# Moving one store to ScalarE's DMA queue, and two new ways to close the output tiles

## The chip, the cores and the metric

The kernel runs on one core of a Trainium2 chip. The metric is device time in microseconds (us). A "span" is the length of the profiled execution from its first to its last record; it is 1.7 to 3.6 us shorter than the device time of the same run in the runs here, mostly about 2. Engines are named as in the profile: PE is TensorE's matmul, PEld its weight load, DVE is VectorE, ACT is ScalarE, POOL is GpSimd, SP is SyncE, and a name with a small q is the engine's own instruction queue.

## The reference, cut to what matters

```python
x = A_x                                                  # 1 x 2048 x 1024, bf16
g = sigmoid((x * gate_w).sum(-1, keepdims=True))
a = irfft2(rfft2(x) * (w_r + 1j * w_i))                  # branch A: a spectral filter
Bu = einsum("bld,pd->blp", x, B_bar)                     # branch B: a diagonal state space
h = scan(h_t = Lam_bar * h_{t-1} + Bu_t)
b = 2.0 * einsum("blp,dp->bld", h, Cmat).real + x * Dskip
return g * a + (1 - g) * b                               # 1 x 2048 x 1024, bf16
```

The output has 16 row tiles of 128 tokens. Branch B's result for the first ten tiles is ready long before branch A's, so it is parked in DRAM (the "early" tiles). The last six are finished in one go (the "own" tiles).

## The kernel before

The **front end** has 16 steps. In each, TensorE turns x (`turn_x`), multiplies it (`fd`), ScalarE evicts it, TensorE multiplies again (`s1`), VectorE (in the last six steps ScalarE) evicts that as A, and A is stored to a DRAM scratch. B and C arrive by DMA transposes of SyncE's queue meanwhile. From step 8 on, products with B come between.

```python
def load_B(jb):
    for ri, src in enumerate((B_B_re, B_B_im)):
        nc.sync.dma_start_transpose(out=BT[jb][:, ri], in_=src[P * jb:P * (jb + 1), :])

def s1(j):
    ...                                                  # four matmuls into psa
    A1 = gta.tile([P, 2, K], BF16, name="A1", bufs=3)
    (nc.vector.tensor_copy if j < 10 else nc.scalar.copy)(out=A1, in_=psa)
    ...
    nc.sync.dma_start(out=turn1_dram[j].rearrange("r m k -> m r k"), in_=A1)
```

The **back end** closes tiles. `spectral` makes branch A's tile in a buffer: eight matmuls, a ScalarE copy and four VectorE steps. Own tiles use the two halves of a buffer called raw in turn; early tiles use the buffers of B, which is no longer needed.

```python
def late_tile(tb, yl):                                   # an early tile; yl was loaded from DRAM
    ga, _ = spectral(tb, gB, flat(BT[4 + tb % 4]))
    nc.vector.tensor_add(out=ga, in0=yl, in1=ga)
    nc.sync.dma_start(out=out2[P * tb:P * (tb + 1), :], in_=ga.rearrange("p h n -> p (h n)"))

def own_tile(tb, ga):
    psy = psA.tile([P, D], FP32, name="ps_y", tag="ps")
    ga, o = ga
    for hf in range(2):
        c_half(psy, tb, hf, ga)                          # product with C; ga joins by an identity matmul
        if hf == 0:
            load_xs(tb + 1)                              # DMA transpose of the next tile's x, on SyncE
            yield "half"
    nc.scalar.activation(out=o..., in_=psy, func=ACT.Copy, scale=omg[:, tb:tb + 1])
    nc.sync.dma_start(out=out2[P * tb:P * (tb + 1), :], in_=o...)
    yield 3.9
```

The order on TensorE, VectorE and ScalarE is as written; that of SyncE and GpSimd is chosen by the scheduler. The scheduler also hands completion semaphores round among the DMAs of SyncE and ScalarE: eight in the traces of the kernel before (100, 102, 103 and 105 to 109).

Of the kernel before, what the change touches and what calls it, by code (L numbers as in the profile page):

```python
# [11 lines left out]
ACT = mybir.ActivationFunctionType  # L12
ALU = mybir.AluOpType
FP32 = mybir.dt.float32
BF16 = mybir.dt.bfloat16
# [5 lines left out]
D = 1024  # L21
K = 512
H = K // 2
P = 128
TC = 256
NCH = S // TC
NEARLY = 10
NHA, NHB = 4, 2

MAGIC = 12582912.0  # L30
# [75 lines left out]
def kernel(  # L106
# [17 lines left out]
    nc = tc.nc  # L124
    x = A_x[0]
    out2 = out[0]
# [12 lines left out]
    turn1_dram = dram.tile([16, 2, P, K], BF16, name="turn1_scratch")  # L139
    turn2_dram = dram.tile([32, P, K], BF16, name="turn2_scratch")  # L140
    col0_dram = dram.tile([P, 16, 2], BF16, name="col0_scratch")
    z_dram = dram.tile([P, 16], FP32, name="z_scratch")
    y_dram = dram.tile([NEARLY, 2, P, K], FP32, name="y_scratch")

# [16 lines left out]
    gta = ictx.enter_context(tc.tile_pool(name="gta", bufs=2, side="right"))  # L161
    psA = ctx.enter_context(tc.tile_pool(name="psA", bufs=2, space=PSUM, reuse_waits="tile"))
# [11 lines left out]
    ident = cpool.tile([P, P], BF16, name="ident")  # L174
# [7 lines left out]
    BT = [btp.tile([P, 2, 8, P], BF16, name=f"BT{jb}") for jb in range(8)]  # L182
# [12 lines left out]
    def load_T3(a, b):  # L195
        nc.sync.dma_start(out=fft["T3"][:, a:b], in_=cT3[:, a:b])

    def load_B(jb):
        for ri, src in enumerate((B_B_re, B_B_im)):
            nc.sync.dma_start_transpose(out=BT[jb][:, ri], in_=src[P * jb:P * (jb + 1), :])  # L200


    def make_tab(jp):
# [32 lines left out]
    hs = {}  # L236
# [85 lines left out]
    def gfnet():  # L322
        T3_sb, G_sb = fft["T3"], fft["G"]
        Acol = fx.tile([P, 16, 2], BF16, name="Acol")
# [11 lines left out]
        def s1(j):  # L336
            X1 = X1s.pop(j)
            psa = psA.tile([P, 2, K], FP32, name="ps_s1", tag="ps")
            nc.tensor.matmul(psa[:, 0, :], lhsT=T3_sb[:, j, 0, :], rhs=X1[:, 0, :], start=True, stop=False)
            nc.tensor.matmul(psa[:, 0, :], lhsT=T3_sb[:, j, 1, :], rhs=X1[:, 1, :], start=False, stop=True)  # L340
            nc.tensor.matmul(psa[:, 1, :], lhsT=T3_sb[:, j, 0, :], rhs=X1[:, 1, :], start=True, stop=False)
            nc.tensor.matmul(psa[:, 1, :], lhsT=T3_sb[:, j, 2, :], rhs=X1[:, 0, :], start=False, stop=True)
            A1 = gta.tile([P, 2, K], BF16, name="A1", bufs=3)
            (nc.vector.tensor_copy if j < 10 else nc.scalar.copy)(out=A1, in_=psa)  # L344
            if j:
                nc.vector.tensor_copy(out=Acol[:, j - 1, :], in_=A1s[j - 1][:, :, 0])
            A1s[j] = A1
            nc.sync.dma_start(out=turn1_dram[j].rearrange("r m k -> m r k"), in_=A1)

        A1s, X1s = {}, {}  # L350
        fft["fd"], fft["s1"] = fd, s1
        yield "front"
        nc.vector.tensor_copy(out=Acol[:, 15, :], in_=A1s[15][:, :, 0])
        nc.gpsimd.dma_start(out=col0_dram, in_=Acol)
        Bcol = fx.tile([P, 16, 2], BF16, name="Bcol")
        with nc.allow_non_contiguous_dma(reason="tiny corner turn"):
# [77 lines left out]
        for h in range(2):  # L434
            for ri in range(2):
                nc.tensor.matmul(qps[:, h, :], lhsT=fft["Sel"][:, 2 * h + ri, :], rhs=Qb[:, :, ri],
                                 start=(ri == 0), stop=(ri == 1))
# [46 lines left out]
        for G in range(8):  # L484
# [3 lines left out]
            for kp in range(2):  # L488
                psz = psA.tile([P, 2, K], FP32, name="ps_is2", tag="ps")
                for kl in range(2):  # L490
                    kc = 2 * kp + kl
                    pv = psz[:, kl, :].rearrange("p (n t) -> p n t", t=8)
                    for g in range(4):
                        nc.tensor.matmul(pv[:, :, g::4], lhsT=Cq[:, g, P * kc:P * (kc + 1)], rhs=KRS_sb[:, 1, :],  # L494
                                         start=True, stop=True)
                nc.scalar.copy(out=ZT[:, 4 * kp:4 * kp + 4, :, 8 * G:8 * G + 8],  # L496
                               in_=psz.rearrange("p kc (r n t) -> p (kc r) n t", r=2, t=8))
# [27 lines left out]

    bctx = ExitStack()
    gen = gfnet()

    def step():
# [10 lines left out]
    xs = {}  # L540

    def load_xs(tb):
        if tb < 16:
            xs[tb] = fft["lp"].tile([P, 8, P], BF16, name="xs", bufs=2)
            nc.sync.dma_start_transpose(out=xs[tb], in_=x[P * tb:P * (tb + 1), :])

    def c_half(psy, tb, dh, ga=None):
        c, tq = tb // 2, tb % 2
        vector_until(c)
        for i in range(16):  # L550
            jb, ri = i // 2, i % 2
            nc.tensor.matmul(psy[:, 512 * dh:512 * (dh + 1)], lhsT=hs[c, jb // 4][:, ri, jb % 4, P * tq:P * (tq + 1)],  # L552
                             rhs=CT[ri][:, jb, 512 * dh:512 * (dh + 1)], start=(i == 0), stop=False)
        for d4 in range(4):
            d8 = 4 * dh + d4
            nc.tensor.matmul(psy[:, P * d8:P * (d8 + 1)], lhsT=xs[tb][:, d8, :],  # L556
                             rhs=fft["dgD"][:, d8, :], start=False, stop=(d4 == 3 and ga is None))
        if ga is not None:
            nc.tensor.matmul(psy[:, 512 * dh:512 * (dh + 1)], lhsT=ident, rhs=ga[:, dh], start=False, stop=True)

    def early(tb):
        psy = pools["u"].tile([P, D], FP32, name="ps_y", tag="psu")
# [11 lines left out]
    own_home = lambda tb: raw[:, 2 * D * (tb % 2):2 * D * (tb % 2 + 1)]  # L574
    flat = lambda t: t.rearrange("p r j m -> p (r j m)")

    def spectral(tb, scale, home):
        ZT_t = fft["ZT"]
        pse = pools["u"].tile([P, 4, H], FP32, name="ps_id", tag="psu")
        for slot, (cls, ri) in enumerate(((0, 0), (1, 1), (0, 1), (1, 0))):  # L580
            for kb in range(2):
                i = 4 * cls + 2 * kb + ri
                nc.tensor.matmul(pse[:, slot, :], lhsT=ZT_t[:, i, tb, :], rhs=fft["Gi"][:, i, :],  # L583
                                 start=(kb == 0), stop=(kb == 1))
        part = home[:, 0:D].rearrange("p (s c n) -> p s c n", s=2, c=2)
        nc.scalar.activation(out=part.rearrange("p s c n -> p (s c) n"), in_=pse, func=ACT.Copy, scale=scale[:, tb:tb + 1])  # L586
        eo = home[:, D:2 * D].rearrange("p (c k) -> p c k", c=2)
        nc.vector.tensor_add(out=eo[:, :, 0:H], in0=part[:, 0], in1=part[:, 1])
        nc.vector.tensor_sub(out=eo[:, :, K - 1:H - 1:-1], in0=part[:, 0], in1=part[:, 1])
        ga = part.rearrange("p s c n -> p s (c n)")  # L590
        nc.vector.tensor_add(out=ga[:, 0], in0=eo[:, 0], in1=eo[:, 1])
        nc.vector.tensor_sub(out=ga[:, 1], in0=eo[:, 0], in1=eo[:, 1])
        return ga, eo

    def late_load(tb):
        yl = flat(BT[tb % 4]).bitcast(FP32).rearrange("p (h n) -> p h n", h=2)
        nc.sync.dma_start(out=yl, in_=y_dram[tb].rearrange("h p n -> p h n"))
        return yl

    def late_tile(tb, yl):  # L600
        ga, _ = spectral(tb, gB, flat(BT[4 + tb % 4]))
        nc.vector.tensor_add(out=ga, in0=yl, in1=ga)
        nc.sync.dma_start(out=out2[P * tb:P * (tb + 1), :], in_=ga.rearrange("p h n -> p (h n)"))

    def own_tile(tb, ga):
        psy = psA.tile([P, D], FP32, name="ps_y", tag="ps")
        ga, o = ga
        for hf in range(2):
            c_half(psy, tb, hf, ga)
            if hf == 0:  # L610
                load_xs(tb + 1)
                yield "half"
        nc.scalar.activation(out=o.rearrange("p h n -> p (h n)"), in_=psy, func=ACT.Copy, scale=omg[:, tb:tb + 1])
        nc.sync.dma_start(out=out2[P * tb:P * (tb + 1), :], in_=o.rearrange("p h n -> p (h n)"))
        yield 3.9


    preTs = {}
# [5 lines left out]
        nc.scalar.copy(out=xQ[:, :, j, :], in_=pt)  # L624

    def fold(j):
        preTs[j] = gta.tile([P, 8, P], BF16, name="preT", bufs=4)
        nc.vector.tensor_add(out=preTs[j][:, 0:4], in0=xQ[:, 0:4, j, :], in1=xQ[:, 4:8, j, :])
        nc.vector.tensor_sub(out=preTs[j][:, 4:8], in0=xQ[:, 0:4, j, :], in1=xQ[:, 4:8, j, :])

    idle = gta.tile([P, K], BF16, name="idle", tag="A1", bufs=3)
    nc.vector.memset(idle, 0.0)

    def keep_warm(n):
# [21 lines left out]
    rows = iter(range(2, 16))  # L656
# [26 lines left out]
    gB = cpool.tile([P, 16], FP32, name="gB")  # L683
    omg = cpool.tile([P, 16], FP32, name="omg")
    grat = cpool.tile([P, 16], FP32, name="grat")
# [34 lines left out]
    def halves(gen, n):  # L720
# [6 lines left out]
                early(8), unit(6, 0), early(9))  # L727

    order = {
        **{j: [(load_B, j - 2)] for j in range(2, 10)},  # L730
        10: [(load_small,)],
        **{j: [(load_C, j - 11)] for j in range(11, 15)},
    }
    at = [0]
# [91 lines left out]
    while at[0] < 16:  # L826
        j = at[0]
# [43 lines left out]
    for _ in ssm:  # L871
        vector(3.5)
    assert step() is None
    yl, ga = {}, {}
    late = list(range(NEARLY))

    def own(tb):
        for v in own_tile(tb, ga.pop(tb)):
            if v == "half" and tb + 1 < 16:
                ga[tb + 1] = spectral(tb + 1, grat, own_home(tb + 1))  # L880
            yield v

    ga[NEARLY] = spectral(NEARLY, grat, own_home(NEARLY))
    for _ in chain(unit(6, 1), unit(7, 0), unit(7, 1)):
        vector(4.0)
    for i in range(4):
        yl[i] = late_load(i)
    for tb, counts in ((10, (0, 0)), (11, (1, 1)), (12, (1, 1)), (13, (1, 1)), (14, (1, 1)), (15, (2, 0))):
        for _, n in zip(own(tb), counts):
            vector(4.0)  # L890
            for _ in range(n):
                i = late.pop(0)
                late_tile(i, yl.pop(i))
                if i + 4 < NEARLY:
                    yl[i + 4] = late_load(i + 4)
    guard.__exit__(None, None, None)


# [28 lines left out]
```

## Time and profile before

| | before |
|---|---|
| device time, median of 3 | 359.76 us (359.44 to 360.09) |
| span | 357.5 us |
| TensorE busy | 342.6 us, 96% |
| VectorE busy | 302.4 us, 85% |
| first product with B starts | 46.94 us |
| second half of it starts | 54.69 us |
| TensorE's last product ends | 352.41 us |

The kernel is close to TensorE's own work. A change can win only what TensorE lacks.

### The profile page before, as it was taken

What the parts mean: (1) busy time and instruction counts of PE and PEld (TensorE: products, weight loads), DVE (VectorE), ACT (ScalarE), POOL (GpSimd) and SP (SyncE); (2) the same over time, 40 slices, a digit from 0 to 9 for tenths busy, and PEclk for the clock granted to TensorE, in tenths of its full rate; (3) what the DMA queues carried; (4) which work ended last, traced back from release to release, by engine and by line L of the source; (5) the groups of instructions that cost most, each with busy time, mean ns of one, the idle gap of its engine ahead of it and who ended that gap; (6) DMA issues with size and microseconds to landing.
All of it is one profiled execution on the core that took longest, in us unless ns stands there. A gap on an engine that the chain in (4) does not pass through costs nothing.

```text
span 357.5 us, 6458 instructions
## 1 busy us (share of the span) xinstructions
PE 342.6 (96%) x2533; PEld 227.8 (64%) x2533; DVE 302.4 (85%) x483; ACT 170.2 (48%) x217; POOL 23.2 (6%) x56
## 2 busy tenths in 40 slices
PE   8989689989999999999999999999999999999994
PEld 4545257757876665665657486597767875665661
DVE  2658385999998999999999999956747998999996
ACT  3698555674432265566646333364423222434432
POOL 1373010120021000000000000000000000000000
PEclk9999989999999999999999999999999999999999
DMA  7999999997592068899999276863203241145673
GB/s 266 415 233 165 239 214 196 225 185 181 185 225 54 38 131 202 213 282 254 253 274 254 82 187 173 200 158 110 88 2 91 64 172 43 33 132 149 206 264 120
DMA packets 83455, 62.18 MB, mean 174 GB/s; under 512 B 54336, under 2 KB 71392, under 8 KB 83296
## 3 DMA queue, kind: packets, MB, share of 16 engines
q1 hardware_dynamic: 82832, 61.70, 67.1%
q0 software_dynamic: 512, 0.05, 0.5%
q8 instruction: 20, 0.33, 0.4%
q14 instruction: 11, 0.09, 0.1%
q10 hardware_dynamic: 80, 0.01, 0.0%
HBM read 31.32 MB, written 17.84 MB: 138 GB/s over the span
## 4 chain that ended last, share of the span: by engine, by line
PE 79%; DVE 7%; ACT 4%; SPq 4%; issue 3%; DMA 3%; ACTq 0%; DVEq 0%
PE ps_y L552 29%; PE psu L295 29%; PE ps_is L494 4%; PE ps_id L583 3%; SPq L200 3%; PE ps_fd L330 3%; PE ps_is L469 2%; PE ps_is L470 2%; PE ps_s L445 2%; PE ps_y L556 2%; DMA G_sb<-c_G 2%; ACT xQ L624 1%; DVE A L344 1%; DMA turn_scratch<-A 1%; ACT h L297 1%
## 5 line engine op out<-in xcount | busy, mean ns | idle before, releaser
L295 PE MATMUL psu<-xQ,BT 128*128 128x256 bf16 x1024 | 117.5, 275 | 1.8 <-ACT zsb L667 1.0
L552 PE MATMUL ps_y<-CT,h 128*128 128x512 bf16 x512 | 115.9, 379 | 0.0
L295 PEld LDWEIGHTS <-BT 128*128 128x128 bf16 x1024 | 101.1, 99 | 18.1 <-issue 2.5
L552 PEld LDWEIGHTS <-h 128*128 128x128 bf16 x512 | 50.2, 99 | 55.2
L269 DVE TENSOR_TENSOR_SCAN h<-rz,h 128x1024 bf16<-128x1024 f32 x32 | 72.3, 2282 | 0.3
L297 ACT CAST h<-psu 128x1024 bf16<-128x1024 f32 x32 | 32.3, 1010 | 60.7 <-PE psu L295 60.7
L256 DVE TENSOR_TENSOR su<-h,tab 128x2048 bf16<-128x2048 bf16 x16 | 19.6, 1223 | 16.4 <-ACT h L297 13.3
L330 PE MATMUL ps_fd<-G_sb,preT 128*128 128x512 bf16 x128 | 30.4, 379 | 0.5 <-ACT X L333 0.3
L570 ACT ACTIVATE ye<-ps_y,omg 128x512 f32<-128x512 f32 x20 | 12.7, 685 | 31.2 <-PE ps_y L556 25.2
L344 DVE CAST A<-ps_s 128x1024 bf16<-128x1024 f32 x10 | 12.2, 1223 | 11.2 <-DMA turn_scratch<-A 6.8
L330 PEld LDWEIGHTS <-preT 128*128 128x128 bf16 x128 | 11.9, 97 | 13.6 <-issue 1.2
L257 DVE TENSOR_TENSOR h<-h,tab 128x2048 bf16<-128x2048 bf16 x16 | 19.6, 1225 | 1.0
L496 ACT CAST ZT<-ps_is 128x1024 bf16<-128x1024 f32 x16 | 15.4, 1020 | 10.3 <-PE ps_is L494 6.7
L333 ACT CAST X<-ps_fd 128x1024 bf16<-128x1024 f32 x16 | 16.2, 1013 | 8.5 <-PE ps_fd L330 8.4
L282 DVE TENSOR_TENSOR h<-h,tab 128x2048 bf16<-128x2048 bf16 x16 | 19.6, 1225 | 0.5
L447 ACT CAST X<-ps_s 128x1024 bf16<-128x1024 f32 x16 | 16.2, 1014 | 7.0 <-PE ps_s L445 7.0
L281 DVE TENSOR_TENSOR sg<-h,tab 128x2048 bf16<-128x2048 bf16 x16 | 19.5, 1219 | 0.1
L472 ACT CAST C<-ps_is 128x1024 bf16<-128x1024 f32 x16 | 16.1, 1007 | 2.8 <-PE ps_is L470 2.8
L624 ACT COPY xQ<-pt 128x1024 bf16<-128x1024 bf16 x16 | 15.9, 1019 | 2.1 <-PE pt L623 2.1
L583 PE MATMUL ps_id<-raw,ZT 128*128 128x256 bf16 x128 | 15.8, 273 | 0.0
L586 ACT ACTIVATE raw<-ps_id,grat 128x1024 bf16<-128x1024 f32 x6 | 6.7, 1114 | 18.1 <-PE ps_id L583 18.1
L494 PE MATMUL ps_is<-KRS_sb,raw 128*128 128x128 bf16 x128 | 15.3, 311 | 0.0
(187 smaller groups left out, 397.4 us busy)
## 6 DMA issues: line engine op xcount, KB each, us to landing
y_scratch<-ye SPq DMA_DIRECT2D x20, 256.0 KB, 2.7
BT<-y_scratch SPq DMA_DIRECT2D x10, 512.0 KB, 4.1
CT<-in_A_x_dram SPq DMA_DIRECT2D x8, 512.0 KB, 6.5
turn_scratch<-A SPq DMA_DIRECT2D x16, 256.0 KB, 2.9
Bb<-turn_scratch SPq DMA_DIRECT2D x16, 256.0 KB, 4.1
turn_scratch<-C SPq DMA_DIRECT2D x16, 256.0 KB, 3.3
raw<-turn_scratch SPq DMA_DIRECT2D x16, 256.0 KB, 4.2
Wb<-in_A_w_r_dram SPq DMA_DIRECT2D x32, 127.8 KB, 4.3
```

Of the source, the lines that this page charges most:

```text
L256: nc.vector.tensor_mul(out=su, in0=u[:, ::-1], in1=bc(1))
L257: nc.vector.tensor_mul(out=u, in0=u, in1=bc(0))
L269: nc.vector.tensor_tensor_scan(out=seg, data0=rz[:, js].rearrange("p j t -> p (j t)"), data1=seg, initial=0.0, op0=ALU.mult, op1=ALU.add)
L281: nc.vector.tensor_mul(out=sg, in0=u[:, ::-1], in1=bc(3))
L282: nc.vector.tensor_mul(out=u, in0=u, in1=bc(2))
L295: nc.tensor.matmul(psu[:, j, :], lhsT=BT[4 * q + j][:, ri, d8, :], rhs=xQ[:, d8, :, 16 * c:16 * (c + 1)], start=(d8 == 0), stop=(d8 == 7))
L297: nc.scalar.copy(out=u[:, ri].rearrange("p b (q j) -> p b q j", j=16), in_=psu.rearrange("p b (j q) -> p b q j", j=16))
L330: nc.tensor.matmul(ps[:, cls, :], lhsT=preTs[j][:, 4 * cls + d4, :], rhs=G_sb[:, cls, d4, :], start=(d4 == 0), stop=(d4 == 3))
L494: nc.tensor.matmul(pv[:, :, g::4], lhsT=Cq[:, g, P * kc:P * (kc + 1)], rhs=KRS_sb[:, 1, :], start=True, stop=True)
L552: nc.tensor.matmul(psy[:, 512 * dh:512 * (dh + 1)], lhsT=hs[c, jb // 4][:, ri, jb % 4, P * tq:P * (tq + 1)], rhs=CT[ri][:, jb, 512 * dh:51 ...
L583: nc.tensor.matmul(pse[:, slot, :], lhsT=ZT_t[:, i, tb, :], rhs=fft["Gi"][:, i, :], start=(kb == 0), stop=(kb == 1))
L624: nc.scalar.copy(out=xQ[:, :, j, :], in_=pt)
```

## The change

Its intent: take the A stores away from SyncE's queue, where they stand between B's transposes; relieve VectorE of the ten late sums; and shorten the end. The diff, cut to its core:

```diff
-    def load_B(jb):
-        for ri, src in enumerate((B_B_re, B_B_im)):
-            nc.sync.dma_start_transpose(out=BT[jb][:, ri], in_=src[...])
+    parts_B = iter([(jb, ri) for q in range(2) for ri in range(2) for jb in range(4 * q, 4 * q + 4)])
+    def load_B(n):
+        for _ in range(n):
+            jb, ri = next(parts_B)
+            nc.sync.dma_start_transpose(out=BT[jb][:, ri], in_=(B_B_re, B_B_im)[ri][...])
...
-            A1 = gta.tile([P, 2, K], BF16, name="A1", bufs=3)
+            A1 = gta.tile([P, 2, K], BF16, name="A1", bufs=4)
...
-            nc.sync.dma_start(out=turn1_dram[j].rearrange("r m k -> m r k"), in_=A1)
+            if j:
+                keep_A1(j - 1)
+        def keep_A1(j):
+            nc.vector.tensor_copy(out=Acol[:, j, :], in_=A1s[j][:, :, 0])
+            nc.scalar.dma_start(out=turn1_dram[j].rearrange("r m k -> m r k"), in_=A1s[j])
...
-    def late_tile(tb, yl):
-        ga, _ = spectral(tb, gB, flat(BT[4 + tb % 4]))
-        nc.vector.tensor_add(out=ga, in0=yl, in1=ga)
-        nc.sync.dma_start(out=out2[...], in_=ga...)
+    def late_tile(tb):
+        ga, _ = spectral(tb, gB, flat(BT[tb % 8]))
+        nc.gpsimd.dma_start(out=ga, in_=y_dram[tb]..., accum_op=ALU.add)
+        closing.append((tb, ga))                         # stored one tile later, from SyncE's queue
...
+        if tb < NSUM:                                    # NSUM = 13: own tiles 10 to 12 as before
...                                                      # own tiles 13 to 15:
         for hf in range(2):
+            psh = psA.tile([P, K], FP32, name="ps_h", tag="ps")
+            c_half(psh, tb, hf)                          # no identity matmul
+            nc.vector.scalar_tensor_tensor(out=o[:, hf], in0=psh, scalar=omg[:, tb:tb + 1], in1=ga[:, hf],
+                                           op0=ALU.mult, op1=ALU.add)
+            nc.sync.dma_start(out=out2[rows, K * hf:K * (hf + 1)], in_=o[:, hf])
...
-        **{j: [(load_B, j - 2)] for j in range(2, 10)},
-        10: [(load_small,)],
+        **{j: [(load_B, n)] for j, n in ((2, 1), (3, 1), (4, 1), (5, 2), (6, 2), (7, 2), (8, 2), (9, 2))},
+        10: [(load_B, 3), (load_small,)],
```

Each A is now stored one step late (`keep_A1(j - 1)`). The cut parts give the turned x one buffer less (preT, 4 to 3) and start the late tiles one own tile earlier.

More of the change, by code (lines that the diff above doesn't have):

```diff
@@ L27 @@
 NEARLY = 10
+NSUM = 13
 NHA, NHB = 4, 2
@@ L196, in load_T3 @@
         nc.sync.dma_start(out=fft["T3"][:, a:b], in_=cT3[:, a:b])
-    def load_B(jb):
-        for ri, src in enumerate((B_B_re, B_B_im)):
-            nc.sync.dma_start_transpose(out=BT[jb][:, ri], in_=src[P * jb:P * (jb + 1), :])
+    parts_B = iter([(jb, ri) for q in range(2) for ri in range(2) for jb in range(4 * q, 4 * q + 4)])
+    def load_B(n):
+        for _ in range(n):
+            jb, ri = next(parts_B)
+            nc.sync.dma_start_transpose(out=BT[jb][:, ri], in_=(B_B_re, B_B_im)[ri][P * jb:P * (jb + 1), :])
     def make_tab(jp):
@@ L342, in s1 @@
             nc.tensor.matmul(psa[:, 1, :], lhsT=T3_sb[:, j, 2, :], rhs=X1[:, 0, :], start=False, stop=True)
-            A1 = gta.tile([P, 2, K], BF16, name="A1", bufs=3)
+            A1 = gta.tile([P, 2, K], BF16, name="A1", bufs=4)
             (nc.vector.tensor_copy if j < 10 else nc.scalar.copy)(out=A1, in_=psa)
+            A1s[j] = A1
             if j:
-                nc.vector.tensor_copy(out=Acol[:, j - 1, :], in_=A1s[j - 1][:, :, 0])
-            A1s[j] = A1
-            nc.sync.dma_start(out=turn1_dram[j].rearrange("r m k -> m r k"), in_=A1)
+                keep_A1(j - 1)
+        def keep_A1(j):
+            nc.vector.tensor_copy(out=Acol[:, j, :], in_=A1s[j][:, :, 0])
+            nc.scalar.dma_start(out=turn1_dram[j].rearrange("r m k -> m r k"), in_=A1s[j])
         A1s, X1s = {}, {}
@@ L352, in gfnet @@
         yield "front"
-        nc.vector.tensor_copy(out=Acol[:, 15, :], in_=A1s[15][:, :, 0])
+        keep_A1(15)
         nc.gpsimd.dma_start(out=col0_dram, in_=Acol)
@@ L547, in c_half @@
     def c_half(psy, tb, dh, ga=None):
+        psy = psy[:, K * dh:K * (dh + 1)] if psy.shape[1] == D else psy
         c, tq = tb // 2, tb % 2
@@ L551, in c_half @@
             jb, ri = i // 2, i % 2
-            nc.tensor.matmul(psy[:, 512 * dh:512 * (dh + 1)], lhsT=hs[c, jb // 4][:, ri, jb % 4, P * tq:P * (tq + 1)],
+            nc.tensor.matmul(psy, lhsT=hs[c, jb // 4][:, ri, jb % 4, P * tq:P * (tq + 1)],
                              rhs=CT[ri][:, jb, 512 * dh:512 * (dh + 1)], start=(i == 0), stop=False)
@@ L555, in c_half @@
             d8 = 4 * dh + d4
-            nc.tensor.matmul(psy[:, P * d8:P * (d8 + 1)], lhsT=xs[tb][:, d8, :],
+            nc.tensor.matmul(psy[:, P * d4:P * (d4 + 1)], lhsT=xs[tb][:, d8, :],
                              rhs=fft["dgD"][:, d8, :], start=False, stop=(d4 == 3 and ga is None))
         if ga is not None:
-            nc.tensor.matmul(psy[:, 512 * dh:512 * (dh + 1)], lhsT=ident, rhs=ga[:, dh], start=False, stop=True)
+            nc.tensor.matmul(psy, lhsT=ident, rhs=ga[:, dh], start=False, stop=True)
     def early(tb):
@@ L593, in spectral, with close @@
         return ga, eo
-    def late_load(tb):
-        yl = flat(BT[tb % 4]).bitcast(FP32).rearrange("p (h n) -> p h n", h=2)
-        nc.sync.dma_start(out=yl, in_=y_dram[tb].rearrange("h p n -> p h n"))
-        return yl
-    def late_tile(tb, yl):
-        ga, _ = spectral(tb, gB, flat(BT[4 + tb % 4]))
-        nc.vector.tensor_add(out=ga, in0=yl, in1=ga)
-        nc.sync.dma_start(out=out2[P * tb:P * (tb + 1), :], in_=ga.rearrange("p h n -> p (h n)"))
+    def late_tile(tb):
+        ga, _ = spectral(tb, gB, flat(BT[tb % 8]))
+        nc.gpsimd.dma_start(out=ga, in_=y_dram[tb].rearrange("h p n -> p h n"), accum_op=ALU.add)
+        closing.append((tb, ga))
+    closing = []
+    def close(keep):
+        while len(closing) > keep:
+            tb, ga = closing.pop(0)
+            nc.sync.dma_start(out=out2[P * tb:P * (tb + 1), :], in_=ga.rearrange("p h n -> p (h n)"))
     def own_tile(tb, ga):
-        psy = psA.tile([P, D], FP32, name="ps_y", tag="ps")
         ga, o = ga
-        for hf in range(2):
-            c_half(psy, tb, hf, ga)
+        rows = slice(P * tb, P * (tb + 1))
+        if tb < NSUM:
+            psy = psA.tile([P, D], FP32, name="ps_y", tag="ps")
+            for hf in range(2):
+                c_half(psy, tb, hf, ga)
+                if hf == 0:
+                    load_xs(tb + 1)
+                    yield "half"
+            nc.scalar.activation(out=o.rearrange("p h n -> p (h n)"), in_=psy, func=ACT.Copy, scale=omg[:, tb:tb + 1])
+            nc.sync.dma_start(out=out2[rows, :], in_=o.rearrange("p h n -> p (h n)"))
+            yield 3.9
+            return
+        for hf in range(2):
+            psh = psA.tile([P, K], FP32, name="ps_h", tag="ps")
[3 more added lines that the diff above has]
+            nc.sync.dma_start(out=out2[rows, K * hf:K * (hf + 1)], in_=o[:, hf])
             if hf == 0:
@@ L612, in own_tile @@
                 yield "half"
-        nc.scalar.activation(out=o.rearrange("p h n -> p (h n)"), in_=psy, func=ACT.Copy, scale=omg[:, tb:tb + 1])
-        nc.sync.dma_start(out=out2[P * tb:P * (tb + 1), :], in_=o.rearrange("p h n -> p (h n)"))
         yield 3.9
@@ L626, in fold @@
     def fold(j):
-        preTs[j] = gta.tile([P, 8, P], BF16, name="preT", bufs=4)
+        preTs[j] = gta.tile([P, 8, P], BF16, name="preT", bufs=3)
         nc.vector.tensor_add(out=preTs[j][:, 0:4], in0=xQ[:, 0:4, j, :], in1=xQ[:, 4:8, j, :])
         nc.vector.tensor_sub(out=preTs[j][:, 4:8], in0=xQ[:, 0:4, j, :], in1=xQ[:, 4:8, j, :])
-    idle = gta.tile([P, K], BF16, name="idle", tag="A1", bufs=3)
+    idle = gta.tile([P, K], BF16, name="idle", tag="A1", bufs=4)
     nc.vector.memset(idle, 0.0)
@@ L873 @@
     assert step() is None
-    yl, ga = {}, {}
+    ga = {}
     late = list(range(NEARLY))
@@ L879, in own @@
             if v == "half" and tb + 1 < 16:
-                ga[tb + 1] = spectral(tb + 1, grat, own_home(tb + 1))
+                ga[tb + 1] = spectral(tb + 1, grat if tb + 1 < NSUM else gB, own_home(tb + 1))
             yield v
@@ L885 @@
         vector(4.0)
-    for i in range(4):
-        yl[i] = late_load(i)
-    for tb, counts in ((10, (0, 0)), (11, (1, 1)), (12, (1, 1)), (13, (1, 1)), (14, (1, 1)), (15, (2, 0))):
+    for tb, counts in ((10, (1, 1)), (11, (1, 1)), (12, (1, 1)), (13, (1, 1)), (14, (1, 1)), (15, (0, 0))):
         for _, n in zip(own(tb), counts):
@@ L891 @@
             for _ in range(n):
-                i = late.pop(0)
-                late_tile(i, yl.pop(i))
-                if i + 4 < NEARLY:
-                    yl[i + 4] = late_load(i + 4)
+                close(1)
+                late_tile(late.pop(0))
+            if tb == 15:
+                close(0)
     guard.__exit__(None, None, None)
```

## The prediction

Two passages with general statements, which no trace of this case shows, are cut from it. No term of its sum stood in them: 359.8 + 8 + 0.7 + 3 - 1.8 = 369.7, and 366.5 after 3.3 is taken back. What it says of semaphores agrees with the trace of the kernel before: of the DMAs of SyncE and ScalarE there, 89 have a predecessor on the same semaphore whose landing the trace tells, and none was issued before that landing. Its 0.22 us for an identity product is the step between 128x512 products in that trace (starts at 41.06, 41.28 and 41.49 us).

> **What bounds the kernel now.** I read the page first: its busy shares, its row for TensorE and its chain of the work that ended last.
>
> ```profile
> span 357.5 us, 6458 instructions
> PE   8989689989999999999999999999999999999994
> PE 79%; DVE 7%; ACT 4%; SPq 4%; issue 3%; DMA 3%; ACTq 0%; DVEq 0%
> ```
>
> TensorE is the chain for 79% of the span and is full from the sixth of the 40 slices (some 9 us each) to the last. Time is to be won only where its row falls short: the first 50 us, the worst being the fifth slice, and the last 5 us. The chain in order of time and TensorE's own timeline tell what it lacks in the fifth slice:
>
> ```profile
> 36.94 0.53 SPq L348
> 37.52 1.28 SPq L200
> 38.84 1.31 SPq L200
> 40.19 1.31 SPq L200
> 41.60 3.09 DMA turn_scratch<-A
> 44.80 1.24 DVE A L344
> 46.08 0.38 PE ps_s L339
> 47.11 5.16 PE psu L295 x32
> ...
> 41.06 0.38 PE L339 MATMUL ps_s<-X,raw 128*128 128x512 bf16 x1 [2.42 <-DVE A L344]
> 46.08 0.38 PE L339 MATMUL ps_s<-X,raw 128*128 128x512 bf16 x1 [2.27 <-DVE A L344]
> ```
>
> The store of the first token result (L348) stands in SyncE's queue behind B's transposes (L200, 1.3 us of issue each). VectorE can't write the next A until an old store has landed, and TensorE waits for VectorE twice. TensorE's real gaps are 38.3 to 41.1 and 43.4 to 46.1, some 5.4 us. The first B product after them took 5.2 us where later ones take 3.5 to 3.7, so about 1.6 us more is a lowered clock (0.85 in that window by the busy time by stage). Together 7 us are at stake here.
>
> At the end the timeline shows the last product stopping at 352.41 us, then eviction, VectorE's sums and stores:
>
> ```profile
> 348.36 3.62 PE L552 MATMUL ps_y<-CT,h 128*128 128x512 bf16 x16
> 352.03 0.38 PE L559 MATMUL ps_y<-raw,ident 128*128 128x512 bf16 x1
> 353.19 1.23 DVE L602 TENSOR_TENSOR BT<-BT,BT 128x1024 bf16<-128x1024 f32 x1
> 354.45 0.33 SPq L603 DMA_DIRECT2D out_dram<-BT x1
> ```
>
> That tail is 357.5 - 352.4 = 5.1 us. The busy time by stage has TensorE at 20.00 of 20 from 280 to 340 us beside VectorE at 18 to 19.5: VectorE is full, but TensorE never waits for it there.
>
> [...] This build has eight hardware-DMA semaphores handed round, and each DMA waits first until the last user of its semaphore has landed. [...] No accumulating DMA is in this trace; its small GpSimd transfers of 8 KB or less land in 4.0 to 6.4 us.
>
> **The change, part by part.**
>
> *Store from ScalarE.* It removes four stores from among B's transposes and gives A four buffers. If nothing else happened, the 5.4 us of gaps and the 1.6 us of clock would be won. It adds 16 issues to ScalarE. At 0.53 us each (SyncE's row for the same transfer), the six or so in the steps before 40 us cost 3.2 us on an engine that is already busy 9.2 and 9.1 us of 10 in the windows 20 to 30 and 30 to 40; some 1.5 us of this finds no slack.
>
> *The new wait.* The instruction order of the built kernel shows which semaphores are handed to whom, and this is where I place the result. The schedule puts all transposes on SyncE far ahead. So ScalarE's store 1 waits for the landing of the 1st of B's 16 transposes, store 2 for the 6th, store 3 for the 10th, store 4 for the 15th, store 5 for the 1st of C's, store 6 for the 6th, store 7 for the 10th. While it waits, ScalarE can neither copy turned x nor evict the FFT products. The landings: inputs occupy the DMA engines to about 21.9 us (the last table was issued at 10.1 and took 11.8), then transposes follow at 1.31 us each with two stalls of some 1 us as before, and each lands some 4 us after its issue (page: 4.2 and 5.5). That gives the 6th at about 31 us, the 10th at 37, the 15th at 43.6, and after the 16th and three small loads C's 1st at 48, its 6th at 54, its 10th at 59.5. ScalarE's work in a step is three casts of 1.0 us plus one issue, 3.6 us (up to 1.3 more with tables). It reaches store 2 at about 28, is held to 31, reaches store 3 at 34.5, held to 37, reaches store 4 at 40.5, held to 43.6. From there two table casts (1.3), three copies (3.0) and store 5 take it to 48.7, the rest of the table (2.6) to 51.3, and the eviction for step 8 to 52.3. TensorE then has fd (1.7) and s1 (0.9) before the first B product, which starts near 54.9 where it now starts at 46.9: 8 us late. Store 6 and 7 hold ScalarE to 54.5 and 60; table work and the eviction of the first B product follow to 63.6, and its second half, with one PSUM buffer, starts there, not at 54.7: 8.9 us late. TensorE is full afterwards (only some 1.8 us of gaps up to 350 us, about 1 of which may absorb delay), so I carry 8 us to the end.
>
> *B in half blocks.* Same 16 transposes, same issue. The first product needs four of them before step 8; they land long before. Worth 0 by itself.
>
> *Early tiles closed by accumulating DMA.* Removes ten sums of 1.225 us, 12.25 us of VectorE, and ten 512 KB loads. TensorE didn't wait for VectorE there, so this is worth nothing on the path until the tail. It adds ten GpSimd transfers. My estimate of one is 6.6 us: about 4.5 for the path as the small ones show, plus some 2 us more for 512 KB (the plain load of that size takes 4.1). SyncE's order now has the next x transpose behind the store of an accumulated tile. From the spectral product to x landed: cast 1.2, four VectorE steps 1.6, its backlog 2, issue 1, accumulation 6.6, issue 0.4, transpose 3.9, 16.7 us; TensorE needs that x about 13.8 us after. So tiles 12 and 14 may each stall by up to 2.9 us; I count 3 us for both, as the backlog is uncertain.
>
> *Last three tiles by VectorE.* Removes six identity products, at 0.22 us of pipelined time each 1.3 us of TensorE, and the 1.11 us cast of 128x1024; a half tile's sum from PSUM is estimated at 0.7 us (ScalarE's cast of this shape takes 0.685). The last half's store would end the kernel some 3.5 us after TensorE rather than 5.1, but it stands behind tile 9's accumulated store, which I expect 3 to 5 us after TensorE's end. I count 1.3 + 0.5 = 1.8 us won.
>
> Sum: 359.8 + 8 + 1.5 (ScalarE issue, half of it already in the steps above, so 0.7) + 3 - 1.8 = 369.7. The holds rest on an assumed pace of transposes that start earlier than now, so I take back about a third of the hold and stall terms (11 x 0.3 = 3.3) and get 366.5.
>
> **The rivals.** *A: the queue is freed and nothing replaces it.* ScalarE reaches its stores after the transposes have landed. Then 7 us in front and 2 us at the end are won, less 1.5 us of issue: about 352. For it: SyncE's queue shrinks by 0.53 us a step and starts B about 3 us earlier. Against it: ScalarE reaches store 2 around 28 us, and six transposes can't land within 6 us of the last input at 1.3 us each. *B: ScalarE's issue is the bound.* No holds, but 0.53 us a step on a 91% engine gives back 3 us of the 7: about 355. *C: ScalarE is held, as above*: 366 to 370. *D: the tail alone goes wrong*, accumulations of 10 us or more holding x and the last store: 5 to 8 us lost at the end, with front gains 357 to 360, with front losses 373. C has the instruction order for it, so I give it about 0.6.
>
> **Range and chances.** C centres near 367, which is just on the 2% line (359.76 x 1.02 = 366.96). A reaches past the other line (352.6) only if nearly all comes true. Predicted 366.5 us, range 355 to 373; faster by over 2% 0.10, within 2% 0.44, slower by over 2% 0.46.
>
> **What would show it.** Right: ScalarE's stores preceded by idle time ended by landings of BT and CT transposes; the first B product near 55 us instead of 46.9; gaps of TensorE between 30 and 65 us of 10 us or more; no wait of VectorE's A for its store. In the tail: TensorE waiting for x at tiles 12 or 14, the accumulating transfers landing in 6 to 7 us, the sums L602 gone, TensorE's last product 4 to 5 us before the end. Wrong: a fifth slice at 9 with ScalarE not waiting before its stores, or a first B product at 42 us or earlier; then A or B holds. If TensorE is late in front by the 8 us and the time is still near 360, the tail won more than I allow.

## The result, and the profile after

The changed kernel took **383.85 us** (median of all four runs; the three fast ones took 383.22, 383.76 and 383.94) against 359.92 for the kernel before on the same chip (four runs). The ratio is 1.0655, with a 95% interval of 1.0623 to 1.0687: slower. Ratios here are the mean time of one kernel's runs over that of the other's in the same rounds, so they are not quite the ratio of the medians quoted. Executions over 1.5% slower than the fastest of the same kernel are left out of the means. The other run of the changed kernel took 1264.08 us, counts as slow and explains nothing below. The profile shown here is of another execution: its span, 379.9 us, is that of none of the four timed runs (1261.9, 381.1, 381.8 and 380.2). No run of any later kernel showed such a time.

Four lines of the page of the kernel after: the span, TensorE's busy tenths in 40 slices (now 9.5 us each), its granted clock in the same slices, and the chain by engine.

```profile
span 379.9 us, 6436 instructions
...
PE   7985576999999899999999999999999999999952
...
PEclk9996879699999999999999999999999999999998
...
PE 53%; DVE 16%; DMA 14%; SPq 10%; ACT 2%; issue 2%; ACTq 0%; DVEq 0%; POOLq 0%
```

The hole in the front end is larger: slices 4 to 7 read 5, 5, 7, 6. The granted clock falls there too (0.73 from 30 to 55 us). A new hole stands in the last two slices (5, 2).

ScalarE's timeline of the same run, with its DMA issues (ACTq). The columns are start, duration, engine, line and operation; the bracket gives the idle time before and what ended it.

```profile
45.59 0.37 ACTq L355 DMA_DIRECT2D turn_scratch<-A  x1
46.00 0.63 ACT L811 ACTIVATE rot_kk<-ang 128x512 f32<-128x512 f32 x1 [4.86 <-DMA BT<-in_B_B_im_dram]
...
63.50 0.39 ACTq L355 DMA_DIRECT2D turn_scratch<-A  x1
63.99 0.72 ACT L814 ACTIVATE cs_f<-rot_kk,chpi 128x512 f32<-128x512 f32 x1 [4.12 <-DMA CT<-in_B_C_im_dram]
```

The issue itself takes only 0.37 to 0.39 us. But ScalarE stood idle for 4.86 and 4.12 us until a transpose of B or C had landed, although neither the store nor the table step after it reads B or C. The other stores of this stretch show the same at 32.23 us (5.39 idle), 37.88 (2.81) and 57.41 (3.76). There the view names a computing engine as the releaser. The semaphore records of the same trace, which no view prints, show what it was: these five stores, at 32.23, 37.88, 45.59, 57.41 and 63.50 us, each start within 0.1 us of the landing of the transpose that used their semaphore before (32.16, 37.81, 45.51, 57.33 and 63.48 us).

TensorE's timeline of the same run, at three products that came late and at the corner turn:

```profile
49.01 3.57 PE L334 MATMUL ps_fd<-G_sb,preT 128*128 128x512 bf16 x8 [5.54 <-ACT X L337]
...
56.69 3.66 PE L299 MATMUL psu<-xQ,BT 128*128 128x256 bf16 x32
...
67.25 6.45 PE L299 MATMUL psu<-xQ,BT 128*128 128x256 bf16 x32 [4.31 <-ACT h L301]
...
125.20 0.17 PE L409 MATMUL zps<-Bcol,K_sb 128*128 128x16 bf16 x1 [2.01 <-DMA Bcol<-col_scratch]
```

The two halves of the first B product in the kernel before:

```profile
46.94 5.32 PE L295 MATMUL psu<-xQ,BT 128*128 128x256 bf16 x32
...
54.69 3.66 PE L295 MATMUL psu<-xQ,BT 128*128 128x256 bf16 x32
```

TensorE waits for ScalarE's evictions, 5.54 and 4.31 us in two of the holds. After both waits the next products also run at a lowered clock: eight fd products take 3.57 us where unheld ones take 1.89 (granted clock 0.51 from 49.0 to 52.6 us), and a half of the B product takes 6.45 instead of 3.66 (0.55 from 67.25 to 73.7 us, against 1.00 in the half from 56.69 us). The times grow by about as much as the clock falls: 3.57 / 1.89 = 1.9 and 6.45 / 3.66 = 1.8. After other waits in these runs the clock did not go by the length of the wait; "Why the prediction was wrong" has them.

The first B product starts 9.75 us later than before (56.69 against 46.94) and its second half 12.6 us later (67.25 against 54.69). That half itself then runs 2.8 us longer (6.45 against 3.66), which makes 15.4. Some 1.2 us are taken up where the kernel before waited too (1.03 us before its product at 75.73 us). At the first product with C the delay is 14.2 us (119.36 against 105.19). Right after it TensorE waits 2.0 us for the corner turn's small transfer (8 KB through DRAM, `Bcol<-col_scratch`), which needs the A results. From there to 280 us the delay stays near 16.3 us.

The back end, in lines from the timelines of SyncE, VectorE and TensorE of the kernel after:

```profile
340.07 4.31 SPq L613 DMA_DIRECT2D out_dram<-BT  x2
344.48 1.76 SPq L552 DMA_TRANSPOSE xs<-in_A_x_dram  x1
346.33 0.53 SPq L626 DMA_DIRECT2D out_dram<-raw  x1
...
364.88 0.43 DVE L596 TENSOR_TENSOR raw<-raw 128x512 bf16<-128x512 bf16 x1 [8.25 <-DMA out_dram<-raw]
...
368.62 3.61 PE L560 MATMUL ps_h<-CT,h 128*128 128x512 bf16 x16 [3.84 <-DVE raw L632]
```

Two stores of accumulated tiles (L613) stand ahead of the next x transpose and the own tile's store (L626). Each waits on SyncE until its accumulation has landed. From 356.6 us VectorE has nothing left that it may do: the buffer raw may not be rewritten before the own store has landed, and it waits 8.25 us. That store (tile 13, second half) was issued at 358.98 us, 4.5 us after its sum was done at 354.5, and landed at 364.76. So it is late with the half sum (L632) that frees PSUM, and TensorE waits 3.84 us. Over all, SyncE waited 39.3 us in these ten stores, VectorE 9.9 us for own stores, and TensorE 4.7 us for half sums.

The sum by place: 16.3 us up to 280 us, then 3.7 more by TensorE's last product (372.45 against 352.41), then 2.35 more in the drain, the time from there to the end (7.45 against 5.1): 22.4 us, the difference of the spans 379.9 and 357.5. The medians differ by 23.9 us, so this profiled execution falls 1.5 us short of the whole loss.

### The profile page after: what moved, and what is told of

Its sections match the earlier page's. It is cut to its first block, busy times and chain, and to the rows that moved or that the text cites. A ratio compares the mean times of both kernels' runs of the same rounds, so it can differ in the third digit from the quotient of the medians.

```text
span 379.9 us, 6436 instructions
## 1 busy us (share of the span) xinstructions
PE 346.8 (91%) x2527; PEld 229.0 (60%) x2527; DVE 294.2 (77%) x479; ACT 167.2 (44%) x214; POOL 35.8 (9%) x66
## 4 chain that ended last, share of the span: by engine, by line
PE 53%; DVE 16%; DMA 14%; SPq 10%; ACT 2%; issue 2%; ACTq 0%; DVEq 0%; POOLq 0%
PE psu L299 23%; PE ps_y L560 18%; SPq L204 8%; DVE h L273 4%; PE ps_is L501 4%; DMA BT<-y_scratch 3%; DMA out_dram<-raw 3%; PE ps_is L476 2%; PE ps_s L452 2%; PE ps_is L477 2%; DMA Bcol<-col_scratch 2%; DMA raw<-c_T 2%; DMA col_scratch<-Acol 2%; DVE h L286 1%; DMA vec<-in_B_log_dt_dram 1%
## 5 line engine op out<-in xcount | busy, mean ns | idle before, releaser
L560 PE MATMUL ps_y<-CT,h 128*128 128x512 bf16 x416 | 94.2, 379 | 0.0
L334 PE MATMUL ps_fd<-G_sb,preT 128*128 128x512 bf16 x128 | 33.7, 409 | 7.4 <-ACT X L337 6.5
L605 POOL DMA_DIRECT2D BT<-y_scratch x10 | 12.1, 1206 | 232.5 <-DVE BT L600 220.7
L334 PEld LDWEIGHTS <-preT 128*128 128x128 bf16 x128 | 12.7, 102 | 22.8 <-issue 11.2
L560 PE MATMUL ps_h<-CT,h 128*128 128x512 bf16 x96 | 21.7, 379 | 4.7 <-DVE raw L632 4.7
L348 DVE CAST A<-ps_s 128x1024 bf16<-128x1024 f32 x10 | 12.2, 1221 | 10.7 <-PE ps_s L346 10.7
L503 ACT CAST ZT<-ps_is 128x1024 bf16<-128x1024 f32 x16 | 15.4, 1020 | 10.3 <-PE ps_is L501 6.7
```

Source lines behind the costliest of these rows:

```text
L334: nc.tensor.matmul(ps[:, cls, :], lhsT=preTs[j][:, 4 * cls + d4, :], rhs=G_sb[:, cls, d4, :], start=(d4 == 0), stop=(d4 == 3))
L560: nc.tensor.matmul(psy, lhsT=hs[c, jb // 4][:, ri, jb % 4, P * tq:P * (tq + 1)], rhs=CT[ri][:, jb, 512 * dh:512 * (dh + 1)], start=(i == 0 ...
```

## The experiments

Twelve kernels ran, all correct. Those of one group ran on the same chip with the same runs of the kernel before. Where a median is compared with one of another group, the kernel before says how far chips differ: 360.08, 359.58, 359.01 and 359.65 us in the four groups. "The new front alone" below is the change's front end with the back end of before.

**front_only: the new front alone.** The edit is the first half of the diff above.

> The changed kernel's first part alone (A stored from ScalarE one step late, four A buffers, B in half blocks); the tail is that of before. If the parts are independent, as I hold, it takes 359.9 + 16.3 = some 376 us, with the first B product near 56.7 us as in the changed kernel. If the 6 us at the end were brought on by the late front (a rival), the whole 24 us would be found here: 382 or more.

Measured: 376.60 us (375.37 to 377.91), ratio 1.0462 (1.0420 to 1.0504). TensorE waited 7.1 us for evictions of fd, 6.5 for turned x and 4.5 for evictions of the B product; ScalarE 5.2 and 3.9 us for transposes of B and C. The front end costs 376.6 - 360.1 = 16.5 us, so it is most of the loss.

**tail_only: the new back end alone**, on the front end of before.

> The changed kernel's last part alone (accumulating transfers and VectorE's sums in the last three tiles); the front is that of before. Independent parts: 359.9 + 6.1 = some 366 us, with the own tile's store again behind accumulated tiles' stores and TensorE waiting 4 to 5 us for the half tiles' sums. If the tail costs only after a late front: 358 to 360. If the 1264 us run comes from the accumulating transfers it can come again only here, not in the front alone.

Measured: 369.37 us, scattered (365.61 to 370.60), ratio 1.0243 (1.0177 to 1.0309), unclear. TensorE waited 4.8 us for half sums and 1.8 for x. In this run the old front end's wait for A stores also was 6.0 us rather than the 5.0 of before. The back end costs something by itself; how much is better read below, under pool_tail.

**front_sync: the new front, but the store on SyncE.**

```diff
-            nc.scalar.dma_start(out=turn1_dram[j]...)
+            nc.sync.dma_start(out=turn1_dram[j]...)
```

> The front alone, but with A stored from SyncE's queue as before (still one step late, four A buffers, B in half blocks). My theory: what costs is ScalarE standing still for semaphores that transposes on the other queue used last. Then this loses nothing: ScalarE is not held, and the fourth buffer even takes away most of the two gaps of before: 354 to 358 us. Rival, that lateness, the half blocks or the smaller preT pool cost the time: it stays near 370 to 376.

Measured: 354.50, 355.12, 360.58 and 361.92 us, the last two slow. The profiled run (354.5) has no waits on ScalarE's evictions over 1.3 us, TensorE waits only 0.3 us for A, and the first B product starts at 43.59 us:

```profile
43.59 3.66 PE L298 MATMUL psu<-xQ,BT 128*128 128x256 bf16 x32
```

So in its two fast runs the new front (fourth A buffer, late step, half blocks) wins some 5 us without another queue, as much as front_pool below. Whether it does so reliably stays open: two of four runs are slow, and their granted clock (0.995 and 0.994) is no lower than that of the kernel before in fast runs on this chip (0.991 to 0.994), so the record doesn't tell whether the chip or a wait of the kernel made them slow.

**front_pool: the new front, but the store on GpSimd.** GpSimd's DMAs have semaphores of their own: in the traces of the kernel before and after, 111 to 118 tell of GpSimd's transfers alone (14 and 24 of them), and none of these uses one of the eight of SyncE and ScalarE.

```diff
-            nc.scalar.dma_start(out=turn1_dram[j]...)
+            nc.gpsimd.dma_start(out=turn1_dram[j]...)
```

> The front alone, but with A stored from GpSimd's queue, which has semaphores of its own and shares none with SyncE's transposes. My theory: no engine that computes is held, so both gaps of before go: 351 to 356 us. Rival, that any second queue beside the transposes fights with them for the DMA engines: the stores land late, VectorE waits for A again, 365 us or more. [...]

Measured: 354.88 us (354.43 to 354.98), ratio 0.9856 (0.9827 to 0.9885): within 2%, but reliably faster than before. TensorE's row and two lines of its timeline:

```profile
PE   7989899899999999999999999999999999999994
...
42.80 3.66 PE L298 MATMUL psu<-xQ,BT 128*128 128x256 bf16 x32
...
48.97 3.65 PE L298 MATMUL psu<-xQ,BT 128*128 128x256 bf16 x32
```

The holes are gone and the first B product starts at 42.80 us, 4.1 us earlier than before. So the new front wins 5 us when ScalarE is left out of it. How much of that is the other queue, and how much the fourth buffer and the late step, isn't shown: front_sync's two fast runs reach the same time with SyncE's queue. The choice of ScalarE costs 376.6 - 354.9 = 21.7 us against it.

**front_probe: an idle store put in ScalarE's place.** front_pool plus 512 bytes per step to a row that nobody reads. This separates the wait from the data that is stored.

```diff
             nc.gpsimd.dma_start(out=turn1_dram[j]...)
+            nc.scalar.dma_start(out=junk_dram[j], in_=A1s[j][0:1, 0, 0:256])
```

> The front end as in the run with GpSimd's queue (354.9 us: the A results leave from GpSimd's queue, one step late, B in half blocks), with one thing added: at each of the 16 steps ScalarE issues a store of 512 bytes to a scratch row nobody reads. In the compiled program these probes have the same waits, in the same places, as the A stores of the change had (a completion semaphore last used by a B or C transpose of SyncE's queue). Theory (ScalarE is held by semaphores it shares with SyncE's transposes; what it stores does not matter): 373 to 378 us, ScalarE's waits of 2.7 to 5.4 us on transposes of B and C back as in the run of the new front alone. Rival 1 (only the cost of issuing on ScalarE, 16 times 0.4 us, partly beside other work): 355 to 359 us. Rival 2 (A's own transfer is late because it leaves from ScalarE's queue): 354 to 356 us.

Measured: 374.33 us (372.65 to 377.88), ratio 1.0399 (1.0361 to 1.0436). ScalarE's timeline shows one of the holds:

```profile
49.37 0.22 ACTq L356 DMA_DIRECT2D junk<-A  x1
49.64 0.63 ACT L796 ACTIVATE rot_kk<-ang 128x512 f32<-128x512 f32 x1 [7.74 <-DMA BT<-in_B_B_im_dram]
```

Sixteen useless stores of 512 bytes, 0.22 us of issue each, cost some 19 us. What they share with the change's stores is the place in ScalarE's program and the waits for semaphores that the compiled program gives them: the probe above starts at 49.37 us, and the view names a transpose of B as what ended the 7.74 us of idle time around it. Both rivals, issue cost and A's own transfer, are out: they allowed at most 359 us.

**front_pairs: the half blocks taken back.** The new front alone, with B in the order and at the steps of before.

```diff
-        **{j: [(load_B, n)] for j, n in ((2, 1), (3, 1), (4, 1), (5, 2), (6, 2), (7, 2), (8, 2), (9, 2))},
-        10: [(load_B, 3), (load_small,)],
+        **{j: [(load_B, j - 2)] for j in range(2, 10)},
+        10: [(load_small,)],
```

> The change's front end alone (376.6 us), but B transposed in the order and at the steps of before (both parts of a block, one block a step from step 2 on); A still stored from ScalarE's queue one step late. Theory (the half blocks are worth next to nothing, the holds on ScalarE are all): 373 to 380 us with waits of ScalarE for transposes of 10 us or more. Rival (the half blocks crowd the transposes in steps 5 to 10 and cause the holds): 365 us or less.

Measured: 374.49 us (373.81 to 379.93, the last slow), ratio 1.0427 (1.0394 to 1.0461). The interval overlaps front_only's. ScalarE was held 5.6 and 5.4 us by transposes of B. The half blocks are not the cause, and beyond the scatter they neither help nor harm.

**pool_tail: the whole change, A stored from GpSimd.**

> The whole change, but the A results stored from GpSimd's queue. Theory (the back end costs some 6 us by itself, whatever the front): 354.9 + 6 = 361 us, 359 to 365, with VectorE waiting 8 to 10 us for a store of its own tile and TensorE 4 to 5 us for VectorE's half sums. Rival (the back end suffered only from the delays of the front): 353 to 356 us.

Measured: 362.22 us (361.32 to 362.48), ratio 1.0073 (1.0048 to 1.0097). That is 7.3 us over front_pool. Two lines of the waits, VectorE's and TensorE's (total, times, longest):

```profile
DVE raw L596 <- DMA out_dram<-raw: 10.7, 2, 9.1
...
PE ps_h L560 <- DVE raw L632: 4.5, 2, 3.7
```

The parts add up: the new front alone, 376.6, plus 7.3 gives 383.9, where the whole change took 383.85. So close an agreement is luck, as front_only's runs alone span 2.5 us; that the parts are independent is shown to within that.

**pool_accum: of the back end only the accumulating DMA** (NSUM = 16), A stored from GpSimd.

> The front end with GpSimd's queue; of the back end's change only the accumulating DMA (the last three tiles are closed by TensorE and ScalarE as before). Theory (stores of accumulated tiles hold SyncE's queue in order, and with it the stores of the own tiles and the x transposes): 358 to 363 us; VectorE waits for the store of its own tile by 5 us or more in all. Rival (the half sums by VectorE are what costs): 353 to 356 us.

Measured: 362.40 us (361.74 to 362.84), ratio 1.0081. VectorE waited 12.3 us for own stores. TensorE then waited 1.6 us and ran its next product in 5.23 us rather than the 3.62 of the half before. The end came 8.2 us after its last product (360.1 - 351.9), as the last two stores of accumulated tiles again stood ahead of the own one. TensorE's wait and its slowed product:

```profile
345.92 0.50 PE L567 MATMUL ps_y<-raw,ident 128*128 128x512 bf16 x1 [1.63 <-DVE raw L599]
346.21 5.23 PE L560 MATMUL ps_y<-CT,h 128*128 128x512 bf16 x16
```

**pool_vec: of the back end only the half sums by VectorE**, with early tiles loaded and added as before, A stored from GpSimd.

> The front end with GpSimd's queue; of the back end's change only the last three tiles closed by VectorE in halves (early tiles loaded and added by VectorE as before). Theory (this part takes away 6 identity products, about 1.3 us, and shortens the end after the last product by some tenths): 352 to 354.5 us. Rival (the half sums are late on VectorE and hold TensorE's PSUM): 357 to 360 us, with TensorE waiting for VectorE's half sums by 3 us or more.

Measured: 360.40 us (360.22 to 360.57), ratio 1.0027. The theory failed and the rival held. Lines from the timelines of TensorE and VectorE:

```profile
326.69 0.39 PE L564 MATMUL ps_h<-dgD,xs 128*128 128x128 bf16 x4
...
329.41 1.23 DVE L610 TENSOR_TENSOR BT<-BT,BT 128x1024 bf16<-128x1024 f32 x1
330.55 0.74 DVE L630 SCALAR_TENSOR_TENSOR raw<-ps_h,omg,raw 128x512 bf16<-128x512 f32 x1
331.35 5.30 PE L560 MATMUL ps_h<-CT,h 128*128 128x512 bf16 x16 [3.40 <-DVE raw L630]
```

The half product is complete by 327.1 us, but VectorE comes to its sum only at 330.55. It was not idle: it worked off late tiles back to back, 19.15 us of the 20 from 320 to 340. TensorE's next half waits 3.40 us and then takes 5.30 instead of 3.62. That is 5.1 of the 5.5 us lost against front_pool.

**pool_owngp: the own tiles' stores moved out of SyncE's queue**, otherwise pool_tail.

```diff
-            nc.sync.dma_start(out=out2[rows, :], in_=o...)
+            nc.gpsimd.dma_start(out=out2[rows, :], in_=o...)
...
-            nc.sync.dma_start(out=out2[rows, K * hf:K * (hf + 1)], in_=o[:, hf])
+            nc.gpsimd.dma_start(out=out2[rows, K * hf:K * (hf + 1)], in_=o[:, hf])
```

> The whole change with the A results stored from GpSimd's queue (362.2 us), and in the back end one edit: the stores of the own tiles leave from GpSimd's queue too, so that they no longer stand in SyncE's queue behind stores of accumulated tiles. Theory (that order on SyncE's queue is what the accumulation costs): VectorE's waits of 10.7 us for own stores fall under 3 us, TensorE's 4.5 us for half sums under 1.5, and the time to 350 to 354.5 us, under the 354.9 of the front end alone because 6 identity products are gone. Rival (the accumulating DMA is slow by itself, or the load on the DMA engines in the last 60 us): 358 to 362 us. Risk: GpSimd's own queue becomes the one in which stores stand behind accumulations, which cost it 1.2 us each.

Measured: 356.79 us (355.98 to 360.34), ratio 0.9954 (0.9900 to 1.0008). TensorE's waits for half sums are gone from the back end, VectorE's for own stores fell from 10.7 to 4.5 us, and TensorE's last product ends at 347.0 us. So the order in SyncE's queue was what held TensorE. But the time is above what I expected, and the timeline shows why:

```profile
344.14 1.34 POOL L605 DMA_DIRECT2D BT<-y_scratch  x1
...
346.61 0.39 PE L564 MATMUL ps_h<-dgD,xs 128*128 128x128 bf16 x4
```

The last accumulation is issued at 344.14 us, and its landing and the store after it end the span at 354.3 us, 7.3 us after TensorE.

**pool_accum_owngp: the same with NSUM = 16.**

> As the run before, but all own tiles closed by TensorE and ScalarE as before the change (362.4 us with own stores on SyncE's queue). Theory: 351 to 355.5 us, and within 2 us of the run with half sums, since VectorE now has time for them. Rival as above: 358 to 362 us.

Measured: 355.57 us (355.18 to 357.75), ratio 0.9913 (0.9877 to 0.9949), against 362.40 with own stores on SyncE. The same edit brings 6.8 us here (6.3 when the kernel before is set equal on the two chips), and the half sums make no difference beyond the scatter.

**pool_mixed: the last two early tiles by VectorE again**, otherwise pool_owngp, with the stores of the early tiles reordered to suit (cut here).

```diff
-    def late_tile(tb):
+    def late_tile(tb, yl=None):
         ga, _ = spectral(tb, gB, flat(BT[tb % 8]))
+        if yl is not None:                               # tiles 8 and 9, loaded two own halves ahead
+            nc.vector.tensor_add(out=ga, in0=yl, in1=ga)
+            nc.sync.dma_start(out=out2[...], in_=ga...)
+            return
```

> The run with own stores from GpSimd's queue (356.8 us), where TensorE is done at 347.0 us but the last two accumulations, issued at 342.5 and 344.1 us, end the span only at 354.3. Edit: the last two early tiles are loaded and added by VectorE as before the change, in time that the other eight accumulations free. Theory (the end is now the drain of the last accumulations): the last store starts within 2 us of TensorE's end, and the time is 352.5 to 355.5 us. Rival (the added loads and VectorE's adds hold half sums again): 356 to 360 us, with a wait of TensorE for half sums of 2 us or more.

Measured: 354.67 us (354.04 to 355.04, six runs), ratio 0.9861 (0.9835 to 0.9887). In its timeline the last store now follows the last product at once:

```profile
347.40 0.39 PE L564 MATMUL ps_h<-dgD,xs 128*128 128x128 bf16 x4
...
348.87 0.54 POOL L643 DMA_DIRECT2D out_dram<-raw  x1 [0.76 <-DVE raw L641]
```

This confirms the drain as the last limit. But the whole reworked back end now only equals the old one on the same front (front_pool, 354.88). Both are 1.4% faster than the kernel before, and what wins lies in the front end: four A buffers, the late step and a store that ScalarE doesn't issue. Which of these is needed isn't shown (see front_sync).

## Why the prediction was wrong

It gave 366.5 us with a range of 355 to 373; 383.85 lies outside. It gave slower by over 2% the largest chance, 0.46. The mechanism of the front end was right and its size was not: 8 us were carried and 16.3 came. The back end was wrong in mechanism as well: 1.2 us were counted and some 6 to 7 came.

- **What bounds the kernel.** Right. TensorE's gaps by the A store were really to be won: front_pool wins 5 us of the 7 named. (Of the "some 5.4 us" of gaps, the lines shown have 2.42 + 2.27 = 4.7 us as waits.)
- **Store from ScalarE, issue cost.** I took 0.53 us an issue; it is 0.37 to 0.41. A small term, as thought.
- **The new wait.** Right in kind, and shown by front_probe: ScalarE is held by semaphores that it shares with SyncE's transposes. The trace has stores 1 to 7 wait for the very transposes that the prediction lists. The mis-sized term was the pace, "transposes follow at 1.31 us each". I had stores 2 to 7 leave at 31, 37, 43.6, 48, 54.5 and 60 us; they left at 32.23, 37.88, 45.59, 50.43, 57.41 and 63.50. From store 3 to 4 the queue advanced five transposes in 7.7 us, 1.5 each. So the first B product came at 56.69 rather than 54.9, and its second half at 67.25 rather than 63.6. The steps after a hold were sized well: from store 4's release to the first B product 11.3 us were counted and 11.1 measured.
- **What was left out of that sum: the clock.** I had read 1.6 us of lowered clock before, yet charged none after the holds I predicted. Two of the late products above alone show (3.57 - 1.89) + (6.45 - 3.66) = 4.5 us of it. Only the second part, 2.8 us, adds to the delay: the first product lies before the first B product, whose lateness the late release explains already. The length of a wait alone did not tell which clock follows. In the kernel after, a wait of 3.84 us was followed by 16 products in 3.61 us (granted clock 1.00 from 368.6 to 372.2 us). But 3.40 us in pool_vec was followed by 16 products in 5.30 us, 1.63 us in pool_accum by 16 in 5.23, and 2.27 us in the kernel before by half a B product in 5.32 us where 3.66 is usual (granted clock 0.68 from 46.9 to 52.3 us).
- **"So I carry 8 us to the end".** This step failed, and the runs show what stood in its place: the second half starts 12.6 us late, not 8.9 (the pace); it runs 2.8 us longer (the clock); 1.2 us are absorbed, as the "about 1" said; and the corner turn, which the sum left out, adds 2.0. That is the 16.3 us of the profile; front_only measured 16.5. Then I took back a third of hold and stall terms for doubt, 3.3 us, in the wrong direction.
- **B in half blocks.** Worth 0 by itself: right within the scatter (front_pairs).
- **Accumulating DMA.** "Worth nothing on the path until the tail" and the 6.6 us were near: in the kernel after, a tile of 128x1024, float32 added onto bf16, took 1.2 us of issue on GpSimd and 5.6 us to land (median of ten). The plain A store of 256 KB landed in 4.9 us from GpSimd (front_pool) and in 3.3 from ScalarE (the kernel after). The step that failed is "the next x transpose behind the store of an accumulated tile", counted at 3 us. In the kernel after, TensorE never waited for x in the back end (1.8 us in tail_only, 0.8 in pool_tail). What stood behind those stores was the own tile's store, and with it the buffer raw, VectorE and the PSUM that VectorE frees. pool_accum_owngp shows it: moving the own stores alone brings 6.8 us.
- **Last three tiles by VectorE.** The half sum's 0.7 us was right (0.74). The six identity products did go, but no run isolates the 1.3 us. "I count 1.8 us won" failed, because I placed a job that TensorE waits for on an engine that I had just called full. pool_vec measures 5.5 us lost in its place. In the whole change the accumulations free VectorE, but then it stands waiting for own stores.
- **The tail's sum.** I had +3 - 1.8 = +1.2 us; pool_tail against front_pool gives +7.3. The drain was named rightly ("behind tile 9's accumulated store") but under-sized: the end came 7.45 us after TensorE, not 3.5 plus a little.
- **Rivals.** C (ScalarE held) was the right one for the front. D's size (5 to 8 us lost at the end) was right for the back, but by luck: it rested on accumulations of 10 us or more, and they landed in 5.6. I treated them as alternatives; they came together, and C with D in my own numbers reaches past the range I gave.

The 1264 us run stays open: it came once in four runs of the changed kernel and in none of the others. tail_only, which has the accumulating transfers too, did not bring it back.

## What to carry to other kernels

Before moving a DMA to a compute engine's queue, list the semaphore waits that the compiled program gives it: in this build ScalarE stopped there for whatever transfer had used the semaphore last, however unrelated, 2.8 to 5.4 us at each of five stores. Before giving TensorE's PSUM to another engine, look at what stands ahead of that job in that engine's order and in the order of its stores, not at the job's own length: in pool_vec TensorE waited 3.40 us for a half sum that took 0.74. Delays from separate causes added up here (376.6 + 7.3 = 383.9 us against 383.85), and a TensorE wait can cost the clock of the next products too (2.8 us after one of 4.31 us here).
